# Token number times one-hot in the routing step, formed from constants in PSUM

## The chip, the cores and the metric

One core of a Trainium2 chip runs the whole program. The metric is device time in microseconds (us) of one execution; the kernel before took 347.86 us (median of 3 runs, 347.45 to 348.50).

## The reference

Three stages follow one another on a sequence of S = 768 tokens.

```python
# 1. attention in hash buckets (8 heads of width 64, six sign projections per head)
q_bits = (np.einsum('bhsd,dk->bhsk', q, proj) > 0).astype(np.int64)
mask = q_bucket[:, :, :, None] == k_bucket[:, :, None, :]
scores = np.where(mask, scale * (q @ k.T), -1e9); attn = softmax(scores); x = attn @ v
# 2. gated MLP (d_model 512, d_ff 1024) that mixes tokens by w_sg
h = gelu(x @ w_in); u, v = h[..., :512], h[..., 512:]
v_s = np.einsum('ts,bsd->btd', w_sg, norm(v) * g_ln) + b_sg
x = x + (u * v_s) @ w_out
# 3. mixture of 8 experts with a sticky choice
for s in range(S):
    fresh_e = int(np.argmax(logits[b, s]))
    e = fresh_e if s == 0 or local_gate[b, s] < 0.5 else prev_e
    prev_e = e
    out[b, s] = p[e] * (np.maximum(x[b, s] @ w1[e], 0.0) @ w2[e])
```

Here p is the softmax of the logits, and an expert that was not chosen adds nothing.

## The kernel before

Tokens lie in six tiles of 128 (one token per partition). Every engine's order of work is written out by hand in text tables (`ATTENTION`, `FEED_FORWARD`, `MIXING`, `EXPERTS`), which a small interpreter walks; engines run their own instructions in that order and wait for each other through semaphores.

The place in question is the mixing stage, table `MIXING`. TensorE interleaves three things there: the token mixing (`mix_mm`, L800, tile `vs`), the output projection (`out_mm`, L823, tile `o`), and the small matmuls of the routing. VectorE adds residuals (L826), gates (L804), splits operands (L815), and runs the routing. ScalarE casts and copies; GpSimd forms the low halves of operands (helper `on_pool`, L215, tiles `x2l`, `wslo` and the weight slabs `w`), in pieces of 128 x 256. SyncE issues the loads of the expert weights (`w_read`, L700, tile `raw`); a raw tile goes through a ScalarE cast (L708) and a subtraction on VectorE (L718) or GpSimd (L215) into one of four slabs.

`route(t)` is a generator per token tile; each entry `route t` of the table runs it up to its next `yield`. It finds the largest logit (L858), builds a key that holds the token's position and expert if the token chooses afresh (L864 to L875), turns the keys into a row in PSUM with TensorE (L878), takes a running maximum over tokens (L880 to L886), and recovers from it `f`, the value by which the reversed expert constants `rev_p` name the expert (L889 to L900). The one-hot row of the token's expert is

```python
nc.vector.tensor_scalar(oh, rev_p, f, None, op0=ALU.is_equal)      # L902
```

`rev_p` is a 128 x 8 piece of the PSUM bank `route_bank`, written once before the stage; the same bank holds the keys' row, the exponentials (L871, ScalarE) and the constants of `pick` (L917). `oh` lies in SBUF (`oh_all`). Later in the route, `what_all[:, t, 0, :]` receives the token number + 1 at the expert's column (L924, the line that changes), and `what_all[:, t, 1, :]` the probability (L928). A matmul (`fill`, L936) sums `what_all` into a table, from which the rows of each expert are gathered. `tok_1` is a column of constants in SBUF (tile `sm`).

After the mixing stage the expert stage begins (first matmul of L1078 at 239.57 us of the span): matmuls L1078 (tile `eh`) and L1110 (tile `y`), with the weights that the stream above prepares.

Of the kernel before, what the change touches and what calls it, by code (L numbers as in the profile page):

```python
# [15 lines left out]
ALU = mybir.AluOpType  # L16
# [168 lines left out]
def kernel(  # L185
# [15 lines left out]
    nc = tc.nc  # L201
# [27 lines left out]
    tok_1 = sm[:, 32:38]  # L229
# [438 lines left out]
    what_all = cpool.tile([P, NT, 2, NE], F32, name="what_all")  # L668
# [54 lines left out]
    with ExitStack() as ctx_b:  # L723
# [109 lines left out]
        def route(t):  # L833
# [54 lines left out]
            f = bp2.tile([P, 1], F32, tag="rf", name="rf")  # L888
# [8 lines left out]
            oh = oh_all[:, t, :]  # L897
# [23 lines left out]
            yield "slot"  # L921
            nc.vector.tensor_scalar_add(se, se, 1e-9)
            yield "se"
            nc.vector.tensor_scalar(what_all[:, t, 0, :], oh, tok_1[:, t:t + 1], None, op0=ALU.mult)  # L924
            yield "id"
            nc.vector.reciprocal(se, se)
            yield "rse"
# [58 lines left out]
        rev_p, iota_p = route_bank[:, P:P + NE], route_bank[:, 2 * P:4 * P]  # L986
        nc.vector.tensor_copy(rev_p, revc)
        nc.scalar.copy(iota_p, iota2)
        routes = [route(t) for t in range(NT)]

        def side_b(name, t, k=0):
# [169 lines left out]
    with tc.If(n_extra > 0):  # L1161
        with ExitStack() as ctx_x:
# [13 lines left out]
            for t in range(NT):  # L1176
# [6 lines left out]
                                        op0=ALU.is_lt, op1=ALU.mult)  # L1183
                nc.vector.tensor_tensor(at[:, 0:1], at[:, 0:1], at[:, 1:2], op=ALU.add)
                nc.vector.scalar_tensor_tensor(ati, rank_all[:, t:t + 1], -float(P), at[:, 0:1],
                                               op0=ALU.add, op1=ALU.add)
# [121 lines left out]
```

## Time and profile before

| | |
|---|---|
| median of 3 runs | 347.86 us (347.45 to 348.50) |
| the profiled execution | 347.92 us, span of its instructions 346.1 us |
| TensorE busy | 324.5 us, 94% |
| VectorE busy | 267.1 us, 77% |
| ScalarE busy | 228.1 us, 66% |
| GpSimd busy | 216.4 us, 63% |
| mean granted TensorE clock | 0.989 |

The span runs from the first to the last instruction of the program. In the profile PE is TensorE, PEld its weight loads, DVE VectorE, ACT ScalarE, POOL GpSimd and SP SyncE; `what_all<-oh_all,sm` names the tile written and the tiles read, and L924 the line of the kernel. The chain of waits follows the work that ended last back to what released it. "Idle before" is the time an engine stood still ahead of an instruction, with what ended it.

### The profile page before, as it was taken

The numbers are of one execution on the slowest core, as the hardware profiler recorded it, in microseconds if no ns is written. First come the engines' busy times: TensorE is split into PE (matmuls) and PEld (weight loads), VectorE is DVE, ScalarE is ACT, GpSimd is POOL, SyncE is SP. The second block draws the span as 40 slices with busy tenths as digits, with TensorE's granted clock in tenths as the row PEclk, the third lists the DMA queues.
The fourth block names the chain that finished last, engine by engine and source line by source line (L and its number), as shares of the span: only waits on it lengthen the run. The fifth ranks groups of instructions, "written<-read, shape, count | busy, mean of one in ns | idle before, by whom it ended". The sixth has DMA issues, their size and how long they took to land.

```text
span 346.1 us, 5609 instructions
## 1 busy us (share of the span) xinstructions
PE 324.5 (94%) x1842; PEld 255.1 (74%) x1842; DVE 267.1 (77%) x524; ACT 228.1 (66%) x403; POOL 216.4 (63%) x314
## 2 busy tenths in 40 slices
PE   6898999999999999999979996989999999999991
PEld 5777687786776676888757784778888888888880
DVE  4896879988898757899964669789849778888723
ACT  3575796778687883589735463537758797688730
POOL 3549948885779547589976697677143440653541
PEclk9999999999999999999999999899999999999997
DMA  7295626334522124140044845258979999899700
GB/s 232 56 320 142 199 63 199 114 68 103 179 48 83 63 67 132 62 167 2 2 165 141 241 146 187 81 202 241 361 272 296 372 357 315 270 327 331 273 19 29
DMA packets 27776, 59.95 MB, mean 173 GB/s; under 512 B 3230, under 2 KB 8094, under 8 KB 27744
## 3 DMA queue, kind: packets, MB, share of 16 engines
q1 hardware_dynamic: 25696, 54.80, 49.1%
q0 software_dynamic: 1120, 3.15, 2.4%
q10 hardware_dynamic: 928, 1.62, 1.5%
q8 instruction: 15, 0.25, 0.3%
q14 instruction: 17, 0.14, 0.1%
HBM read 52.28 MB, written 3.67 MB: 162 GB/s over the span
## 4 chain that ended last, share of the span: by engine, by line
PE 68%; DVE 18%; POOL 5%; issue 3%; DMA 3%; ACT 1%; POOLq 0%; DVEq 0%; ACTq 0%
PE y L1110 13%; PE eh L1078 13%; PE po L490 7%; PE vs L800 7%; PE t L474 6%; PE o L823 4%; PE s L456 3%; PE s L459 3%; PE hv L317 3%; DVE nb_all L463 2%; PE hT L1089 2%; DMA b<-q 2%; DVE q L447 1%; PE pj L440 1%; POOL b L215 1%
## 5 line engine op out<-in xcount | busy, mean ns | idle before, releaser
L708 ACT CAST w<-raw 128x1024 fp32r<-128x1024 f32 x64 | 65.7, 1054 | 11.9 <-DMA raw<-in_w 7.3
L215 POOL TENSOR_TENSOR w<-raw,w 128x256 fp32r<-128x256 f32 x68 | 50.7, 779 | 36.0 <-ACT w L708 36.0
L718 DVE TENSOR_TENSOR w<-raw,w 128x1024 fp32r<-128x1024 f32 x47 | 57.2, 1257 | 4.6 <-ACT w L708 4.6
L467 ACT ACTIVATE e<-s,nb_all 128x768 f32<-128x768 f32 x48 | 43.5, 907 | 17.5 <-DVE nb_all L463 16.1
L463 DVE TENSOR_REDUCE nb_all<-s 128x1 f32<-128x768 f32 x48 | 45.5, 952 | 9.4 <-PE s L459 8.8
L480 ACT COPY pt<-t 128x512 f32<-128x512 f32 x72 | 40.3, 588 | 11.7 <-PE t L474 11.3
L474 PE MATMUL t<-ident,e 128*128 128x128 f32 x288 | 39.8, 274 | 0.4 <-ACT pt L480 0.2
L474 PEld LDWEIGHTS t<-ident,e 128*128 128x128 f32 x288 | 33.7, 140 | 6.9 <-issue 2.3
L490 PE MATMUL po<-pt,vt 128*64 128x384 f32 x192 | 34.7, 495 | 0.0
L1110 PE MATMUL y<-w,hh 128*128 128x512 f32 (+1 forms) x144 | 33.5, 371 | 0.6 <-ACT y L1119 0.6
L456 PE MATMUL s<-k,q 128*128 128x384 f32 x96 | 28.3, 375 | 0.4 <-ACT e L467 0.4
L1110 PEld LDWEIGHTS y<-w,hh 128*128 128x128 f32 x144 | 24.6, 188 | 4.8 <-ACT y L1119 0.8
L800 PE MATMUL vs<-vn,wshi 128*128 128x512 f32 x72 | 25.4, 414 | 1.9 <-ACT wshi L791 1.9
L459 PE MATMUL s<-k,q 76*128 76x384 f32 x96 | 25.4, 343 | 1.0 <-DVE q L447 0.7
L1122 POOL DMA_INDIRECT out<-y,dst_row x8 | 11.2, 1399 | 23.9 <-DVE y L1117 11.3
L1078 PE MATMUL eh<-w,xh 128*128 128x512 f32 x96 | 24.5, 396 | 0.0
L490 PEld LDWEIGHTS po<-pt,vt 128*64 128x64 f32 x192 | 12.3, 136 | 14.3 <-issue 14.1
L215 POOL TENSOR_TENSOR b<-r,k 64x256 fp32r<-64x256 f32 x21 | 15.9, 780 | 10.0 <-DVE k L384 10.0
L317 PE MATMUL h<-w_in_s,xTs 128*128 128x512 f32 x96 | 22.1, 389 | 0.0
L317 PEld LDWEIGHTS h<-w_in_s,xTs 128*128 128x128 f32 x96 | 18.0, 188 | 3.7
L1078 PEld LDWEIGHTS eh<-w,xh 128*128 128x128 f32 x96 | 17.7, 188 | 3.6
L215 POOL TENSOR_TENSOR cv_w<-cv_w,cv_a 128x256 f32<-128x256 f32 x24 | 17.8, 763 | 2.9 <-PE hv L317 2.0
(212 smaller groups left out, 747.3 us busy)
## 6 DMA issues: line engine op xcount, KB each, us to landing
raw<-in_w SPq DMA_DIRECT2D x64, 512.0 KB, 5.4
r<-in_qk SPq DMA_DIRECT2D x7, 768.0 KB, 4.7
raw<-in_w_in SPq DMA_DIRECT2D x8, 512.0 KB, 5.5
wsr<-in_w_sgT SPq DMA_DIRECT2D x6, 384.0 KB, 3.6
raw<-in_w_out SPq DMA_DIRECT2D x4, 512.0 KB, 5.6
vt<-in_v_tok ACTq DMA_DIRECT2D x1, 1536.0 KB, 12.1
xd<-x SPq DMA_DIRECT2D x6, 256.0 KB, 4.6
b<-q SPq DMA_DIRECT2D x7, 192.0 KB, 4.6
```

Source lines behind the costliest of these rows:

```text
L215: nc.gpsimd.tensor_tensor(out[at], a[at], b[at], op=op)
L317: nc.tensor.matmul(ps, a[:, kc, ts_], w_in_s[:, b, kc, ns], start=(kc == 0 and i == 0), stop=(kc == 3 and i == 2))
L463: nc.vector.tensor_reduce(nb_all[:, h, t:t + 1], ss[h, t][:, :, :HALF], axis=AX.XY, op=ALU.max, negate=True)
L467: nc.scalar.activation(e, ss.pop((h, t))[:, :, :HALF], AF.Exp, bias=nb_all[:, h, t:t + 1], accum_out=rs_all[:, h, t:t + 1])
L474: nc.tensor.transpose(ps[:, j * P:(j + 1) * P], es[h, t].rearrange("p g q -> p (g q)")[:, k * P:(k + 1) * P], ident)
L480: nc.scalar.copy(pts[h][:, 4 * i:4 * i + 4, :].rearrange("p b q -> p (b q)"), tps.pop((h, i)))
L490: nc.tensor.matmul(po[j * D:(j + 1) * D, :HALF], vt[:, kt, h * D:(h + 1) * D], pt.rearrange("p (t k) q -> p k t q", k=NT)[:, kt, j * 3:(j ...
L708: nc.scalar.copy(slabs_of[i, e][:, 0, q * 2:(q + 1) * 2, :], raws[part])
L718: nc.vector.tensor_tensor(lo, raw, hi, op=ALU.subtract)
L800: nc.tensor.matmul(ps, a[:, kc, :], b[:, kc, :], start=(k == 0), stop=(k == 17))
L1078: nc.tensor.matmul(ps[e, n], a[:, kc, :], slabs_of[1, e][:, b, kc * 2 + n, :], start=(k == 0), stop=(k == 11))
L1110: nc.tensor.matmul(yb[e][:, cs], a[:, kc, :], slabs_of[2, e][:, b, kc, cs], start=(k == 0), stop=(k == 23))
```

## The change

One line of `route` reads other operands. Instead of multiplying the stored one-hot by the token number, it compares the expert constants with `f` again and multiplies the result by the token number, in one instruction with two per-partition scalars:

```diff
             yield "se"
-            nc.vector.tensor_scalar(what_all[:, t, 0, :], oh, tok_1[:, t:t + 1], None, op0=ALU.mult)
+            nc.vector.tensor_scalar(what_all[:, t, 0, :], rev_p, f, tok_1[:, t:t + 1], op0=ALU.is_equal, op1=ALU.mult)
             yield "id"
```

It runs six times, once per token tile. The order of instructions on all five engines stays as it was, and so do the semaphores that each waits for. On VectorE, in the routes of tiles 1 and 2, the place reads so (`rf` is `f`, `sm` holds `tok_1`, `lg` the logits):

```order
@@ -295,5 +295,5 @@
 L922 TENSOR_SCALAR se<-se 128x1
 L804 SCALAR_TENSOR_TENSOR g<-vs_2293,bsg,u_2_2031 128x512
-L924 TENSOR_SCALAR what_all<-oh_all,sm 128x8
+L924 TENSOR_SCALAR what_all<-route_bank,rf,sm 128x8
 L858 TENSOR_REDUCE rmx<-lg_2474 128x1
```

Only the operands of the third instruction differ: its one tensor input now comes from PSUM.

## Rows read from the trace of the kernel before

**Rows 1.** The page: span, and busy time of TensorE.
```profile
span 346.1 us, 5609 instructions
PE 324.5 (94%) x1842; PEld 255.1 (74%) x1842; DVE 267.1 (77%) x524; ACT 228.1 (66%) x403; POOL 216.4 (63%) x314
```

**Rows 2.** Busy time by stretch: stretch; PE, PEld, DVE, ACT, POOL; clock, DMA share, GB/s.
```profile
205.00:210.00 5.00, 5.00 (x34) 3.56 (x32) 3.78 (x17) 2.42 (x4) 5.00 (x9) 1.00 0.82 248
210.00:215.00 5.00, 1.94 (x12) 1.40 (x12) 4.96 (x10) 1.13 (x4) 3.36 (x5) 1.00 0.59 239
215.00:220.00 5.00, 5.00 (x21) 3.69 (x19) 3.52 (x17) 2.79 (x5) 4.18 (x6) 0.66 0.01 2
```

**Rows 3.** The chain that ended last, 206 to 217 us: start, us, what.
```profile
206.16 0.44 PE x2T L837 x4
...
209.98 3.41 DVE what_all L924
...
214.55 0.32 PE route_bank L878
214.87 1.61 PE vs L800 x6
216.48 0.85 PE x2T L837 x4
```

**Rows 4.** VectorE in order of time: start, us, line, op, tiles, shapes.
```profile
206.55 0.23 DVE L902 TENSOR_SCALAR oh_all<-route_bank,rf 128x8 f32<-128x8 f32 x1
...
209.90 3.49 DVE L924 TENSOR_SCALAR what_all<-oh_all,sm 128x8 f32<-128x8 f32 x1
213.30 0.15 DVE L858 TENSOR_REDUCE rmx<-lg 128x1 f32<-128x8 f32 x1
...
221.32 0.22 DVE L924 TENSOR_SCALAR what_all<-oh_all,sm 128x8 f32<-128x8 f32 x1
```

**Rows 5.** GpSimd in order of time: start, us, ..., x count, [idle before].
```profile
209.19 1.44 POOL L215 TENSOR_TENSOR x2l<-x,x2h 128x256 fp32r<-128x256 f32 x2
210.57 2.79 POOL L215 TENSOR_TENSOR w<-raw,w 128x256 fp32r<-128x256 f32 x4
215.30 2.88 POOL L215 TENSOR_TENSOR x2l<-x,x2h 128x256 fp32r<-128x256 f32 x4 [1.94 <-ACT x2h L960]
...
220.06 2.81 POOL L215 TENSOR_TENSOR w<-raw,w 128x256 fp32r<-128x256 f32 x4
...
227.34 1.41 POOL L215 TENSOR_TENSOR x2l<-x,x2h 128x256 fp32r<-128x256 f32 x2 [4.48 <-ACT x2h L960]
```

**Rows 6.** TensorE in order of time around its longest wait.
```profile
209.73 0.28 PE L851 MATMUL lg<-cst,lts 128*128 128x9 f32 x2
...
211.09 0.39 PE L800 MATMUL vs<-vn,wshi 128*128 128x512 f32 x1
214.55 0.32 PE L878 MATMUL route_bank<-ident,key 128*128 128x128 f32 x1 [3.06 <-DVE what_all L928]
```

**Rows 7.** VectorE by source line: count, duration in ns (least, median, most).
```profile
L924 DVE TENSOR_SCALAR what_all<-oh_all,sm x6: 222/258/3491, 201.2 to 238.2; 128x8 f32<-128x8 f32 x6
...
L902 DVE TENSOR_SCALAR oh_all<-route_bank,rf x6: 216/226/227, 197.1 to 236.6; 128x8 f32<-128x8 f32 x6
...
L898 DVE TENSOR_SCALAR ohb_all<-route_bank,rf,pm x6: 274/276/283, 196.6 to 236.0; 128x8 bf16<-128x8 f32 x6
...
L398 DVE TENSOR_SCALAR q<-r x7: 519/560/1020, 13.4 to 97.6; 128x768 fp32r<-128x768 f32 x7
```

**Rows 8.** ScalarE in order of time, behind the stall.
```profile
213.87 0.24 ACT L871 ACTIVATE route_bank<-lg,nmx 128x8 f32<-128x8 f32 x1 [4.72 <-DVE nmx L867]
```

**Rows 9.** The expert stage: waits of SyncE's queue from 180 us on.
```profile
SPq L700 <- DVE w L718: 44.8, 38, 4.2
SPq L700 <- POOL w L215: 33.2, 14, 3.9
```

**Rows 10.** The expert stage: one weight subtraction on VectorE and the matmuls that use it.
```profile
284.94 3.48 DVE L718 TENSOR_TENSOR w<-raw,w 128x1024 fp32r<-128x1024 f32 x3
...
286.89 2.44 PE L1078 MATMUL eh<-w,xh 128*128 128x512 f32 x10
```

## The prediction

> **What bounds the kernel now.** I read the page first. The span is 346.1 us and TensorE is busy for 94% of it [rows 1], so the kernel is bound by TensorE nearly everywhere, and an instruction on another engine is worth something only where TensorE stands still behind it. The changed line runs six times on VectorE, so the next view is its duration by source line: least 222 ns, median 258 ns, but most 3491 ns [rows 7]. One of six executions took some fifteen times as long as the others. VectorE in order of time shows which: the one that starts at 209.90 us; the next instruction begins at 213.30 us [rows 4].
>
> Did anybody wait for it? The chain of waits says yes: it holds L924 for 3.41 us and goes on to the matmul L878, which turns the next token tile's keys [rows 3]. In the order of TensorE that matmul has an idle gap of 3.06 us ahead of it, ended by VectorE (by L928, which stands a few short instructions behind L924) [rows 6]. Behind the gap there is a second loss, which the busy times by stretch show: from 215 to 220 us TensorE is busy all the time, but the granted clock is 0.66 of full speed, while it is 1.00 in the stretches before [rows 2]. A group of four transposes took 0.44 us at 206 us and 0.85 us at 216 us [rows 3]. So the engine ran part of this stretch at its lower level, 1.2 in place of 2.4 GHz, after standing idle.
>
> **Why the instruction took so long.** It waits on no semaphore, and its work is 128 x 8 numbers. What else happened? GpSimd ran six subtractions back to back, two from 209.19 us and four from 210.57 us to 213.36 us [rows 5], and L924 ended at 213.39 us (209.90 + 3.49), that is, as GpSimd fell idle. L924 reads one tensor from SBUF and writes SBUF, and so does L398, whose longest execution is 1020 ns against a median of 560 [rows 7]. The comparison L902 has the same 128 x 8 shape and reads its tensor from PSUM: 216 to 227 ns in all six cases [rows 7], the one at 206.55 us among them [rows 4], although GpSimd is busy without a break from 205 to 210 us [rows 2]. I take it that L924 stood in line behind GpSimd for a path into SBUF which a read from PSUM does not need. The Trainium skill, "VectorE: DVE Perf Modes", section "Why PSUM operands drop a tier", says that an instruction of this kind uses both SBUF read ports only if its tensor is not in PSUM, and so that PSUM halves its rate in fp32; the rows of L902 show no loss at eight columns.
>
> **The change, part by part.**
>
> *The new instruction.* It is a comparison of 128 x 8 numbers from PSUM with two per-partition scalars. The trace does not have it, but two neighbours: L902 with one such scalar, 226 ns, and L898 with two, 276 ns [rows 7]. I take 0.28 us, as it has two. The other five lose at most 0.28 - 0.22 = 0.06 us each, mostly beside TensorE's work; I count 0.05 us, as if one of them lay on the path. If it were free, the gain below would be 0.19 us larger; if the stall stayed, nothing would be won.
>
> *The stall.* From the start of L924 to that of L858 were 213.30 - 209.90 = 3.40 us [rows 4]. With an instruction of 0.28 us, whose last 0.09 us the next one overlaps as it does now (209.90 + 3.49 - 213.30), it is 0.19 us, so VectorE goes on 3.21 us earlier, at 210.09. L858 also needs the logits from TensorE, which end at 210.01 (209.73 + 0.28) [rows 6], so it is just not held up. ScalarE's exponential sat idle for 4.72 us until VectorE's result came [rows 8] and moves along. The matmul L878 then starts at 214.55 - 3.21 = 211.34 us. The matmul ahead of it started at 211.09 [rows 6], and six of its kind took 1.61 us behind the gap [rows 3], 0.27 us each, so TensorE passes from one to the other with next to no gap. **Term 1: 3.21 us.**
>
> *The clock.* With no gap of 3.06 us there is no reason seen in the trace for the clock to fall. From 215 to 220 us it gave back 5.00 x (1.00 - 0.66) = 1.70 us less work than at full speed [rows 2], and the work is the same. **Term 2: 1.70 us**, between 0, if something else lowered the clock, and 1.70.
>
> *What comes late next.* GpSimd's four subtractions end at 213.36 us as before; its next ones, at 215.30 us, had waited 1.94 us for ScalarE [rows 5], so they come only 1.94 us earlier, while the others come 4.9 us earlier. But GpSimd had another idle gap of 4.48 us at 227.34 us [rows 5]; the lag of about 3 us is gone there, and nothing of it reaches the end. The weight stream of the expert stage is close behind TensorE: three subtractions of weights run from 284.94 us, 1.16 us each, so the first is done at 286.10 and the second at 287.26, and TensorE begins to use them at 286.89 us [rows 10]. There is less than 1 us of room, so the stream must come earlier too. I think that it does: its loads wait 44.8 us and 33.2 us in all for VectorE's and GpSimd's subtractions, which free the buffers [rows 9]; hardly anything in it goes by a fixed time.
>
> *Sum.* 3.21 + 1.70 - 0.05 = 4.86 us. The profiled execution took 347.92 us, 0.06 us above the median of the runs, so the forecast is 347.92 - 4.86 = **343.1 us**.
>
> **The rivals.** A measurement of this kernel can tell about 0.3%, here 1.0 us, from no change.
>
> *The stall goes, and the expert stage takes part of it back.* If GpSimd's late share decided what the weight stream can do, only its 1.94 us would remain: 347.92 - 1.94 = 346.0 us. For it speaks the small room [rows 10]; against it the 4.48 us of idle time in between [rows 5]. Chance 0.07.
>
> *The stall is not what I think, and stays for the most part.* Had L924 only waited for the one subtraction that ran when it came, it would have been free by 210.6 us, after some 0.7 us (2.79 us for four [rows 5]); and at 221.32 us it took just 0.22 us with GpSimd at work from 220.06 us on [rows 4, 5]. Then 3.49 - 0.22 - 0.70 = 2.57 us have another cause, perhaps the writing of `what_all`, which the change keeps. At most 0.70 us is won: 347.2 us or more, no change that can be told. The Trainium skill, "SBUF — State Buffer", section "SBUF: two separate sides", has the rule behind this: VectorE and GpSimd lock a shared pair of ports, and the one that comes first keeps it for the whole of its instruction. By that rule the wait would be one subtraction long; this trace has one that spanned five, so rule and row agree on the two engines, not on the length. For my reading speaks that the stall ends within 0.03 us of the end of GpSimd's run. Chance 0.08.
>
> *Slower.* TensorE arrives early at the expert stage and the weights don't, since their transfers set the pace: the end then stays where it is, and TensorE takes its idle time there. If that is one wait about as long as the 3.06 us, the clock falls after it as it does now and costs 1.70 us more with no work ahead to hide it: 347.92 + 1.70 = 349.6 us. It decides from the point where the weights come no earlier at all; the loads that wait for buffers [rows 9] speak against it. Chance 0.03.
>
> **How the numbers follow.** My forecast has 0.82. The low end takes the whole 3.40 us, 1.70 us, and the distance of the fastest run from the median, 0.41 us: 347.92 - 5.51 = 342.4 us. The high end is Term 1 alone, with the clock not coming back, and 0.58 us for the slowest run above the profiled one: 347.92 - 3.21 + 0.58 = 345.3 us. It covers the forecast's own spread and leaves out the rivals, 0.18 together. Faster by over 0.3%: 0.82 + 0.07 = 0.89; the same 0.08; slower 0.03.
>
> **What the profile afterwards would show.** L924 near 0.28 us in all six cases, the one beside GpSimd's run among them. The matmul L878 with no gap ahead of it near 211.3 us. A granted clock of 1.00 in all stretches from 205 to 230 us, and four transposes at 0.44 us. The first matmul of L1078 some 4.9 us earlier, and no new waits of TensorE for weights behind it. I am wrong if a long instruction of VectorE stands at the same place (another cause), if the gap is there but ends with another engine, or if TensorE's time is won at 215 us and lost again behind 240 us.

## The result, and the profile after

The kernel with the change takes **344.13 us** (median of 6 runs, 343.06 to 345.58), beside 348.15 us for the kernel before on the same chip (6 runs, 346.53 to 349.28). The ratio is 0.989, with a 95% interval of 0.986 to 0.992: **faster by 1.1%**. A second comparison on another occasion gave 344.17 against 348.40 us, a ratio of 0.989 (0.985 to 0.994). The forecast of 343.1 us lies 1.0 us below the median, inside its range.

The profiled execution of the changed kernel took 343.06 us, which is the fastest of its six; its span is 341.3 us. From one profiled execution to the other, as the sum was made, that is 347.92 - 343.06 = 4.86 us. The medians differ by 4.0 and 4.2 us, 0.6 to 0.8 us less; experiment 5 looks for that rest and finds only a part of what may cause it. That the two profiles differ by the sum to the hundredth is partly luck: the six executions lie up to 2.52 us apart, and the profiled one is the fastest of them.

The page of the changed kernel, to be read beside [rows 1]:

```profile
span 341.3 us, 5609 instructions
...
PE 323.7 (95%) x1842; PEld 254.7 (75%) x1842; DVE 263.8 (77%) x524; ACT 228.1 (67%) x403; POOL 217.3 (64%) x314
```

As many instructions on each engine as before, VectorE 3.3 us less busy, and TensorE's share a point up. VectorE by source line:

```profile
L924 DVE TENSOR_SCALAR what_all<-route_bank,rf,sm x6: 276/278/280, 201.2 to 233.5; 128x8 f32<-128x8 f32 x6
```

All six executions take 0.28 us, the long one of 3491 ns [rows 7] is gone, and the others differ little: before, in order of time, they took 0.41, 0.22, 0.29, 0.22 and 0.22 us, so three cost some 0.06 us more than they did and two less. VectorE and TensorE in order of time, at the place of [rows 4] and [rows 6]:

```profile
209.88 0.28 DVE L924 TENSOR_SCALAR what_all<-route_bank,rf,sm 128x8 f32<-128x8 f32 x1
210.08 0.16 DVE L858 TENSOR_REDUCE rmx<-lg 128x1 f32<-128x8 f32 x1
```

```profile
211.07 0.39 PE L800 MATMUL vs<-vn,wshi 128*128 128x512 f32 x1
211.32 0.32 PE L878 MATMUL route_bank<-ident,key 128*128 128x128 f32 x1
```

VectorE starts L924 at the same moment as before (209.88 against 209.90 us) and reaches L858 at 210.08 in place of 213.30 us. TensorE's matmul of the keys has no bracket behind it any more, that is, no idle time ahead of it; it starts 214.55 - 211.32 = 3.23 us earlier. Was GpSimd still at work beside it? Yes, and longer than before, without a break until 220.37 us (217.50 + 2.87):

```profile
210.56 2.84 POOL L215 TENSOR_TENSOR w<-raw,w 128x256 fp32r<-128x256 f32 x4
213.33 4.25 POOL L215 TENSOR_TENSOR x2l<-x,x2h 128x256 fp32r<-128x256 f32 x6
217.50 2.87 POOL L215 TENSOR_TENSOR w<-raw,w 128x256 fp32r<-128x256 f32 x4
...
222.55 1.41 POOL L215 TENSOR_TENSOR x2l<-x,x2h 128x256 fp32r<-128x256 f32 x2 [2.18 <-ACT x2h L960]
```

The 1.94 us that GpSimd waited at 215.30 us [rows 5] have closed, because its work for `x2l` is now ready when the weights are done. The later wait, 4.48 us before, is 2.18 us: GpSimd's lag was taken up in it. Busy time by stretch, beside [rows 2] (stretch; PE, PEld, DVE, ACT, POOL; clock, DMA share, GB/s):

```profile
205.00:210.00 5.00, 5.00 (x33) 3.55 (x32) 3.78 (x17) 2.42 (x4) 5.00 (x9) 1.00 0.79 266
210.00:215.00 5.00, 5.00 (x29) 3.90 (x30) 4.67 (x25) 3.92 (x8) 5.00 (x8) 1.00 0.58 229
215.00:220.00 5.00, 5.00 (x33) 3.58 (x32) 4.32 (x18) 2.75 (x6) 5.00 (x8) 1.00 0.40 129
```

TensorE is busy throughout where it had 1.94 us of work in 5, and its clock stays at 1.00 where it was 0.66 (it is 1.00 in the stretches up to 240 us as well). Last, the waits of TensorE from 200 us to the end (engine, what it began, what released it: us in all, times, longest), and the first matmuls of the expert stage by source line:

```profile
PE route_bank L878 <- ACT x2t L839: 0.7, 1, 0.7
PE y L1110 <- ACT y L1119: 0.6, 1, 0.6
PE pc L1130 <- ACT y L1119: 0.6, 1, 0.6
PE rk L907 <- DVE ohb_all L898: 0.3, 1, 0.3
PE x2T L837 <- DVE x L826: 0.2, 1, 0.2
```

```profile
L1078 PE MATMUL eh<-w,gxhi x32: 387/393/478, 234.7 to 251.4; 128*128 128x512 f32 x32
```

No wait for L928 and none for a weight slab is left or added. The expert stage begins at 234.7 us, and before it began at 239.4 us in the same view; its last matmul of this group moved by the same 4.7 us. What was won at 215 us was kept to the end of the span (346.1 - 341.3 = 4.8 us).

### The profile page after: what moved, and what is told of

It is laid out like the page before. It is cut to its first block, busy times and chain, and to the rows that moved or that the text cites. A ratio compares the mean times of both kernels' runs of the same rounds, so it can differ in the third digit from the quotient of the medians.

```text
span 341.3 us, 5609 instructions
## 1 busy us (share of the span) xinstructions
PE 323.7 (95%) x1842; PEld 254.7 (75%) x1842; DVE 263.8 (77%) x524; ACT 228.1 (67%) x403; POOL 217.3 (64%) x314
## 4 chain that ended last, share of the span: by engine, by line
PE 66%; DVE 17%; POOL 9%; issue 4%; ACT 2%; DMA 1%; POOLq 0%; DVEq 0%; ACTq 0%
PE y L1110 13%; PE eh L1078 13%; PE vs L800 7%; PE po L490 7%; PE t L474 5%; PE o L823 4%; PE hv L317 3%; PE s L456 3%; PE s L459 3%; DVE nb_all L463 2%; POOL q L405 2%; PE hT L1089 2%; POOL b L215 2%; POOL r L404 2%; DVE k L449 1%
## 5 line engine op out<-in xcount | busy, mean ns | idle before, releaser
L215 POOL TENSOR_TENSOR w<-raw,w 128x256 fp32r<-128x256 f32 x68 | 52.7, 812 | 33.3 <-ACT w L708 33.3
L1122 POOL DMA_INDIRECT out<-y,dst_row x8 | 9.8, 1230 | 26.0 <-DVE y L1117 12.7
L456 PEld LDWEIGHTS s<-k,q 128*128 128x128 f32 x96 | 15.0, 189 | 6.4 <-ACT e L467 5.2
```

Source lines behind the costliest of these rows:

```text
L215: nc.gpsimd.tensor_tensor(out[at], a[at], b[at], op=op)
L456: nc.tensor.matmul(s[:, j, :HALF], q1[:, ts_], k1[:, j * HALF:(j + 1) * HALF], start=True, stop=False)
```

## The experiments

My theory: the read of an SBUF tensor makes this small VectorE instruction stand behind GpSimd; the PSUM source removes that, and what TensorE gets back is the gap and the lowered clock behind it.

**1. The same instruction with its constants from SBUF.** `revc` holds in SBUF (tile `sm`) the numbers that `rev_p` holds in PSUM. Everything else, the two scalars and the two operations among it, is the change's.

```diff
-    nc.vector.tensor_scalar(what_all[:, t, 0, :], rev_p, f, tok_1[:, t:t + 1], op0=ALU.is_equal, op1=ALU.mult)
+    nc.vector.tensor_scalar(what_all[:, t, 0, :], revc, f, tok_1[:, t:t + 1], op0=ALU.is_equal, op1=ALU.mult)
```

> The same comparison with two per-partition scalars, but the expert constants are read from SBUF (tile sm) and not from PSUM; all else as in the change. If the read from SBUF is what put the instruction in line behind GpSimd, the tile 1 instruction takes about 3.5 us again, TensorE has its gap of about 3.1 us, and the time is that of before, about 348 us. If the stall hung on the stored one-hot or on the form of the old instruction, it stays away and the time is that of the change, 343 to 344.5 us.

Measured: 350.34 us against 349.08 us for the kernel before, ratio 1.003 (1.001 to 1.006). The stall is back in full. VectorE by source line, then VectorE and TensorE in order of time:

```profile
L924 DVE TENSOR_SCALAR what_all<-sm,rf x6: 280/360/3479, 201.4 to 239.1; 128x8 f32<-128x8 f32 x6
```

```profile
210.08 3.48 DVE L924 TENSOR_SCALAR what_all<-sm,rf 128x8 f32<-128x8 f32 x1
```

```profile
214.72 0.32 PE L878 MATMUL route_bank<-ident,key 128*128 128x128 f32 x1 [3.04 <-DVE what_all L928]
```

So it is neither the operand `oh`, nor the form of the instruction, nor its output `what_all`: with all else the same, the side from which the tensor is read decides between 0.28 and 3.48 us at this place. It is not enough by itself, since the other five read SBUF too and took no more than 0.83 us (one of them, at 235.74 us); experiment 4 is about that. The shortest of the six took 280 ns, as long as the change's from PSUM: what lengthens the instruction by 0.06 us is its second scalar, not PSUM. The profile also has a clock of 0.75 from 240 to 245 us, which the kernel before does not have; whether that is why the median is a little above that of before was not tested.

**2. Tile 1 alone, then tiles 1 and 2.** The long instruction was that of tile 1. The first kernel changes that one only, the second those of tiles 1 and 2:

```diff
+    if t == 1:                       # second kernel: t in (1, 2)
+        nc.vector.tensor_scalar(what_all[:, t, 0, :], rev_p, f, tok_1[:, t:t + 1], op0=ALU.is_equal, op1=ALU.mult)
+    else:
+        nc.vector.tensor_scalar(what_all[:, t, 0, :], oh, tok_1[:, t:t + 1], None, op0=ALU.mult)
```

> The new instruction in the route of tile 1 alone; the other five are the old ones. If the one stalled execution is the whole gain, the time is that of the change, 343 to 344.5 us. If the other five matter, at most 0.06 us each were lost or won by them, so nothing that can be told; a time more than 1 us from that of the change would speak against both.

Measured: 348.79 us, ratio to before 0.999 (0.996 to 1.001). Nothing is won, which no theory had said. VectorE, GpSimd and TensorE of this kernel in order of time:

```profile
211.38 0.28 DVE L925 TENSOR_SCALAR what_all<-route_bank,rf,sm 128x8 f32<-128x8 f32 x1
...
218.03 3.81 DVE L927 TENSOR_SCALAR what_all<-oh_all,sm 128x8 f32<-128x8 f32 x1
```

```profile
219.01 2.80 POOL L215 TENSOR_TENSOR w<-raw,w 128x256 fp32r<-128x256 f32 x4
```

```profile
222.88 0.30 PE L878 MATMUL route_bank<-ident,key 128*128 128x128 f32 x1 [2.52 <-ACT route_bank L871]
```

Tile 1's instruction (L925) is short, but now tile 2's (L927) arrives some 3 us earlier than it did [rows 4], while GpSimd is in a run without a break, and stands until 218.03 + 3.81 = 221.84 us; GpSimd's run ends at 219.01 + 2.80 = 221.81 us. TensorE's gap has moved one tile on (it reads `ACT` because ScalarE's exponential stands between the two), and the clock falls behind it (0.73 from 225 to 230 us). In the kernel before, GpSimd had stood still twice between the two tiles' instructions (1.94 us [rows 5] and the 0.49 us below), and tile 2's, at 221.32 us, came through in 0.22 us although GpSimd was at work again:

```profile
218.67 1.43 POOL L215 TENSOR_TENSOR x2l<-x,x2h 128x256 fp32r<-128x256 f32 x2 [0.49 <-ACT x2h L960]
```

> The new instruction in the routes of tiles 1 and 2, the old one in the other four. With tile 1 alone changed, the long wait came back at tile 2 and the time with it. If these two executions are all that matters, the time is that of the change beside it, within 1 us. If a third old instruction gets the long wait once tile 2 is freed, the time is that of before.

Measured: 345.25 us against 348.40 us, ratio 0.990 (0.987 to 0.993), inside the interval that the whole change had beside the same runs (0.985 to 0.994). The median is 1.1 us above the change's, a little over the 1 us named; its profiled execution has a lowered clock at 180 us, of which experiment 5 tells. The four old instructions that are left take at most 424 ns. So two of the six carry the gain, as far as the intervals can tell, and tile 1 alone is not enough. Tile 2 alone was not run; as its old instruction took 0.22 us in the kernel before, nothing suggests that it would be.

**3. Is lateness all that the stall costs?** The change keeps its PSUM source, and ahead of tile 1's instruction VectorE gets copies of 128 x 256 numbers from PSUM into a spare SBUF tile, seven in the first kernel and three in the second. They read no tensor from SBUF. (The line that makes the spare tile `dly` is left out here.)

```diff
+    if t == 1:
+        for _ in range(7):           # second kernel: 3
+            nc.vector.tensor_scalar(dly, iota_p, 1.0, None, op0=ALU.mult)
```

> The change, with seven dummy copies of 128 x 256 from PSUM on VectorE ahead of the tile 1 instruction, about 7 x 0.46 = 3.2 us, which touch nothing that GpSimd needs. If the cost was only that VectorE came late, the gap of TensorE (about 3.1 us), the low clock behind it (1.7 us) and the time of before come back: about 348 us. If the fight over SBUF cost something beyond the delay, the time stays below, 344 to 346 us.

Measured: 349.08 us, ratio 1.001 (0.999 to 1.003): the kernel is as slow as before. TensorE in order of time, and busy time by stretch:

```profile
214.62 0.32 PE L878 MATMUL route_bank<-ident,key 128*128 128x128 f32 x1 [2.94 <-DVE what_all L931]
```

```profile
215.00:220.00 5.00, 5.00 (x21) 3.74 (x19) 3.60 (x17) 2.87 (x5) 4.11 (x6) 0.66 0.00 0
```

> As the run with seven dummy copies, but with three, about 1.4 us. TensorE then stands still for about 1.4 us. If the clock falls after a gap of this length too, the time is about 1.4 + 1.7 us above the change, 346 to 347.5 us; if it does not, 1.4 us above it, 344.5 to 346 us.

Measured: 346.21 us, ratio 0.991 (0.988 to 0.994). The same two views:

```profile
214.42 0.32 PE L878 MATMUL route_bank<-ident,key 128*128 128x128 f32 x1 [1.11 <-DVE what_all L931]
```

```profile
215.00:220.00 5.00, 5.00 (x35) 3.47 (x35) 4.58 (x20) 2.94 (x6) 4.97 (x8) 1.00 0.02 5
```

A gap of 2.94 us made by idle copies brings the gap of the kernel before, the clock of 0.66 behind it and the whole price. With a gap of 1.11 us the time lies in the range that was named for a lowered clock (346 to 347.5 us), but the clock behind the gap is 1.00: the lowered stretch of this profile is another one, from 180 us (experiment 5). Without its 1.7 us the profiled execution of 346.14 us would have taken some 344.4 us, an estimate, 1.4 us above the change's 343.06. So the short gap costs about its own length and no clock. Nothing beside VectorE's lateness is needed to explain the price of the stall, within the 0.9 us that the first interval leaves.

**4. How long does an SBUF read stand behind GpSimd?** In the first kernel tile 1's instruction of the kernel before, with its old operands, moves ahead of the gating instruction (L804), so that it comes while GpSimd is still at the run's first pieces:

```diff
             nc.vector.tensor_scalar_add(se, se, 1e-9)
+            if t == 1:
+                nc.vector.tensor_scalar(what_all[:, t, 0, :], oh, tok_1[:, t:t + 1], None, op0=ALU.mult)
             yield "se"
-            nc.vector.tensor_scalar(what_all[:, t, 0, :], oh, tok_1[:, t:t + 1], None, op0=ALU.mult)
+            if t != 1:
+                nc.vector.tensor_scalar(what_all[:, t, 0, :], oh, tok_1[:, t:t + 1], None, op0=ALU.mult)
```

> The kernel before with the old instruction of tile 1 alone moved ahead of the gating, some 1.4 us earlier; GpSimd works without a break from before it to 213.4 us. If the instruction waits until GpSimd has no more work, it takes 4.5 us or more, the gating waits behind it, and the time is 348 us or above. If it waits for one GpSimd instruction at most and the long wait was a matter of the moment, it takes 0.2 to 0.9 us and the time is that of the change, 343 to 345 us.

Measured: 349.17 us against 348.63 us, ratio 1.004 (0.999 to 1.009). VectorE in order of time:

```profile
209.23 0.81 DVE L924 TENSOR_SCALAR what_all<-oh_all,sm 128x8 f32<-128x8 f32 x1
...
217.29 3.85 DVE L927 TENSOR_SCALAR what_all<-oh_all,sm 128x8 f32<-128x8 f32 x1
```

Here tile 1's instruction came through after 0.81 us, although GpSimd ran on without a break from 199.53 to 221.10 us; tile 2's then stood 3.85 us, until 221.14 us, with a gap of TensorE of 2.56 us behind it. So the duration is the one named for a wait of one GpSimd instruction, while the time is that of before, because the stall moved to tile 2 as in experiment 2. The wait is not always as long as GpSimd's run. Two kernels, which compute nothing of the reference, measure it by itself. The first repeats 96 rounds of six GpSimd subtractions, with one small VectorE instruction that arrives at a moment which moves on by small steps; the second has GpSimd's work in three groups that ScalarE releases, as in the kernel, with loads of 512 KB running beside every other round.

> No part of the reference is computed: GpSimd runs six subtractions of 128 x 256 back to back in each of 96 rounds, and VectorE puts one small instruction beside them, at moments that move by 33 or 67 ns from round to round: one tensor from SBUF with 8 columns (behind a plain copy, or behind a gating like the one in the kernel), 9 columns, 1 column, two tensors from SBUF, one tensor from PSUM. If the wait lasts one GpSimd instruction, the SBUF forms take 0.2 to 0.9 us, depending on the moment. If it can last as long as GpSimd has work without a break, some take 2 us and more, and end with GpSimd's run. The PSUM form stays at 0.28 us in all rounds under both.

VectorE by source line (L57 comes directly behind an instruction with one PSUM and one SBUF tensor, L59 to L67 behind a copy from PSUM to SBUF):

```profile
L57 DVE TENSOR_SCALAR res<-c,col x24: 218/510/793, 10.6 to 463.5; 128x8 f32<-128x8 f32 x24
...
L59 DVE TENSOR_SCALAR res<-c,col x24: 216/442/812, 5.7 to 458.8; 128x8 f32<-128x8 f32 x24
...
L61 DVE TENSOR_SCALAR res<-pbank,col x12: 271/276/278, 15.3 to 333.7; 128x8 f32<-128x8 f32 x12
...
L63 DVE TENSOR_TENSOR res<-c x12: 157/406/594, 20.1 to 338.5; 128x8 f32<-128x8 f32 x12
...
L65 DVE TENSOR_SCALAR res<-c,col x12: 199/203/206, 24.9 to 343.4; 128x1 f32<-128x1 f32 x12
```

> No part of the reference is computed. As the first probe, with the form of one SBUF tensor and 8 columns alone, but nearer to the place in the kernel: GpSimd does ten subtractions in three groups, each released by a cast of ScalarE, and in every other round three loads of 512 KB run beside them. In the first probe no wait was longer than one GpSimd instruction. If the groups or the transfers make the wait run on, some instructions take 2 us and more (in all rounds, or in those with loads alone). If not, all stay under 0.9 us, and what makes the wait in the kernel last is neither of them.

```profile
L66 DVE TENSOR_SCALAR res<-c,col x32: 220/430/818, 8.0 to 243.4; 128x8 f32<-128x8 f32 x32
```

From PSUM the eight columns always take 271 to 278 ns. From SBUF they take 0.2 to 0.8 us, as the moment falls within a GpSimd instruction of some 0.7 us; two SBUF tensors wait too, and one column never does. With and without loads it is the same. But no round of either kernel waits longer than one GpSimd instruction, and so **what lets the wait run over five of them in the kernel stays open**. Four such waits were seen (3.49, 3.48, 3.81 and 3.85 us), and each ended within 0.05 us of the end of GpSimd's run.

The traces hold a lead. In the profiles of before and of the kernels that keep SBUF reads on this line there are 27 such instructions; the other 23 took at most 0.83 us. All four long ones came when GpSimd had worked for at least 11.1 us without a break (16 instructions or more), all the others after 10.9 us or less (15 or fewer). With its tensor from PSUM, and after as long a run, the instruction took 0.28 us (tiles 1 and 2 in the second kernel of experiment 2). The measuring kernels' runs are six and ten instructions long and could not bring this out. No run tests whether it is the cause.

**5. Where executions of one kernel differ, and a better version.** The change ran again, with a profile of its own:

> The changed kernel once more, unaltered, in more runs beside the kernel before, for a narrower interval and a second profile. The sum gives 4.9 us, a ratio of 0.986; the first comparison gave 0.989 (0.9855 to 0.9924). If the sum holds, the ratio comes out between 0.984 and 0.988; if part of the gain is taken back in most executions, between 0.988 and 0.992, and a profile of a longer execution shows where.

This profiled execution took 344.77 us, 1.71 us more than the first. Both have the same idle gap ahead of a matmul at 179 us; only behind it do they differ. First execution of the changed kernel, TensorE and the stretch after it:

```profile
179.06 0.96 PE L800 MATMUL vs<-vn,wshi 128*128 128x512 f32 x3 [1.94 <-ACT wshi L791]
```

```profile
180.00:185.00 5.00, 5.00 (x28) 4.11 (x27) 2.58 (x3) 2.30 (x4) 2.61 (x4) 1.00 0.47 160
```

Second execution:

```profile
179.10 0.97 PE L800 MATMUL vs<-vn,wshi 128*128 128x512 f32 x3 [1.93 <-ACT wshi L791]
```

```profile
180.00:185.00 5.00, 5.00 (x21) 4.11 (x20) 2.58 (x3) 1.87 (x3) 2.63 (x4) 0.66 0.51 167
```

The lowered clock costs 5.00 x (1.00 - 0.66) = 1.70 us there, which is the difference of the two executions. The gap at 179 us has nothing to do with the change, and was in the kernel before as well:

```profile
179.06 0.97 PE L800 MATMUL vs<-vn,wshi 128*128 128x512 f32 x3 [1.94 <-ACT wshi L791]
```

Of the nine profiles with this gap (1.91 to 1.94 us) four have a lowered clock behind it: this one, tile 1 alone, tiles 1 and 2, and the three copies. The profiled execution of the kernel before and the first of the changed one do not have it, while the medians hold executions of both kinds.

Does that explain why the medians gained 0.6 to 0.8 us less than the sum? Not by itself, since executions of the kernel before can lose the same 1.7 us. Of the change's twelve executions, those eight with a mean granted clock of 0.993 or more took 343.06 to 344.67 us, with a median of 343.65, which is still 0.5 us above the forecast; the other four, at 0.989 or less, took 344.54 to 348.37 us. And the kernel before has executions of 346.38 to 346.85 us with a mean clock of 0.991 to 0.997, above the 0.989 of its profiled one: these lost less to the clock, perhaps nothing behind the stall, so that there was less to give back. No profile of one is at hand, and that part stays open.

Who makes the gap? ScalarE in order of time, first execution:

```profile
177.88 0.38 ACT L988 COPY route_bank<-cst 128x256 f32<-128x256 f32 x1 [4.53 <-DVE route_bank L987]
178.19 0.83 ACT L791 CAST wshi<-wsr 128x768 fp32r<-128x768 f32 x1
```

The cast that TensorE waits for (L791) stands in ScalarE's queue behind a copy of constants into `route_bank` (L988), which has waited 4.53 us for VectorE to write the same bank. The constants can come later, as the next kernel shows. The better version is the change with that copy moved behind the cast:

```diff
         nc.vector.tensor_copy(rev_p, revc)
-        nc.scalar.copy(iota_p, iota2)
...
             elif name == "gated":
+                if t == 0:
+                    nc.scalar.copy(iota_p, iota2)
```

> The change, with one ScalarE copy (the constants of pick, L988), which waits 4.5 us for VectorE at the start of the mixing stage, put behind the cast of the mixing weights (L791) on which TensorE waits 1.9 us at 177 to 179 us. If that wait is what makes executions of the change differ (behind it the clock falls in some and not in others, 1.7 us), the wait is gone, no execution has a low clock from 180 to 185 us, and the median is 2 to 3.5 us below that of the change, 340.5 to 342.5 us, ratio to before 0.978 to 0.983. If the weights' transfer ends last there, not the copy, the wait stays and so does the time, 343.4 to 344.8 us.

Measured: **342.04 us** (5 runs, 341.94 to 342.88) against 348.62 us, ratio 0.981 (0.979 to 0.984), outside the change's intervals. Busy time by stretch, where the kernel with the change alone had 3.06 us of TensorE from 175 to 180 us:

```profile
175.00:180.00 5.00, 4.91 (x20) 3.14 (x20) 4.33 (x7) 1.76 (x3) 4.89 (x6) 1.00 0.68 253
180.00:185.00 5.00, 5.00 (x27) 4.15 (x26) 2.63 (x3) 2.67 (x4) 2.23 (x4) 1.00 0.53 183
```

The gap is gone, and no clock is lost behind it in this profile, the only one of this kernel (of its slowest run, 342.88 us). The median is 2.1 us below the change's, and all five runs are below the fastest of the change's (343.06 us). The gap itself was 1.94 us, so how much of this is the clock cannot be told from the medians.

## Why the prediction was right

**The stall (Term 1, 3.21 us).** Right. L878 starts 3.23 us earlier. The cause was put down to a path into SBUF that a read from PSUM does not need, from the neighbour L902 and from the moment at which the stall ended; experiment 1 shows it, as the SBUF source alone brings 3.48 us back. The rival that put most of the stall down to something else, such as the writing of `what_all`, falls with it: that kernel writes the same output as the change. The row that spoke for this rival, tile 2's 0.22 us beside GpSimd at work, was a real warning all the same, and belongs to the open question of experiment 4.

**The length of the stall.** The rival drew on the rule of the Trainium skill, "SBUF — State Buffer", section "SBUF: two separate sides", that the engine which comes first keeps the shared ports for one instruction. The 104 rounds of the two measuring kernels that read eight or nine columns, or two tensors, from SBUF agree with it (at most 0.82 us), and the kernel's four long waits do not. The prediction needed only that the wait was there and that PSUM avoids it; its words "stood in line behind GpSimd" say no more than is shown.

**The clock (Term 2, 1.70 us).** Right in kind, slightly large. The next tile's matmul of the keys (L878) starts at 218.70 us and started at 223.50 us before, 4.80 us earlier; that is 1.57 us more than the 3.23 us at tile 1's, and the clock's stretch lies between the two. Experiment 3 shows the cause: the gap made by other work lowers the clock in the same way.

**The new instruction (0.28 us, 0.05 us lost).** 276 to 280 ns, as forecast, and no loss that can be seen in the time. The forecast gave it 0.28 us for its second scalar, and experiment 1 bears that out: from SBUF, with two scalars, the shortest took 280 ns. The loss of rate that the prediction cites from the Trainium skill, "VectorE: DVE Perf Modes", section "Why PSUM operands drop a tier", shows in none of these rows at eight columns.

**What comes late next.** Right: GpSimd's lag ended in its later idle time (4.48 us became 2.18 us), no wait for weights appeared, and the expert stage came 4.7 us earlier. The rival that let the expert stage take a part back, and the slower one, both needed weights that stay where they are; they didn't.

**What it missed.** It treated the other five instructions as a cost only, 0.05 us. Experiment 2 shows that with tile 1 alone changed the gain would have been nothing: tile 2's old instruction then meets GpSimd at its new, earlier time. The sum held because the change covers all six. And it took the profiled execution for a typical one, 0.06 us from the median of three runs; on the five occasions the medians of the kernel before were 0.2 to 1.2 us above that execution (348.15 to 349.08 us), and its executions differ in how much clock they lose. That the median came out 1.0 us above the forecast is in part the lowered clock at 180 us, which some executions have; the rest is open (experiment 5).

## What to carry to other kernels

Look at the longest execution of a line, not only at its median, when a small VectorE instruction lies on the path and GpSimd runs beside it; if its operand also lies in PSUM, reading it there cost nothing that could be seen at eight columns and took the instruction out of GpSimd's way. Change all instructions of the kind at once: taking one stall away can move the next one under the same run, as it did here. Take a sum worked out from one execution as a sum for that execution, and look at how far others of the same kernel lie from it. And when a gap of TensorE has ended, look for the price of the clock behind it before counting only the gap.

## What the runs showed of the hardware that was not expected

- A VectorE instruction that reads eight columns from SBUF never waited for more than one GpSimd instruction in the measuring kernels (0.82 us at most), and for five in the kernel (3.48 to 3.85 us, in 4 of 27 cases; the others 0.83 us at most). The four came after 11.1 us or more of GpSimd's work without a break, the others after 10.9 us or less; no run tests whether that is what makes the difference.
- With one column from SBUF the same instruction never waited (199 to 206 ns in 12 rounds beside GpSimd).
- The same idle gap of TensorE, 1.93 and 1.94 us, was followed by a granted clock of 0.66 in one execution and of 1.00 in the other, and by a lowered clock in four of nine profiles in all. After gaps of 2.94 to 3.06 us at 214 us it was 0.66 in each profile (three), and after one of 1.11 us it was 1.00 (one).
